# A written order of tasks for a sparse attention and expert kernel, with transposes of probabilities moved to SP from pair 23 on

## The chip, the cores and the metric

The kernel runs on one core of a Trainium2 chip. A core has TensorE (PE, matmuls, with weight loads shown as PEld), VectorE (DVE), ScalarE (ACT), GpSimd (POOL), and SyncE (SP), which here only issues DMAs. The engines run side by side, each in the order of its own program, and wait for each other through semaphores. Matmul results go to PSUM, which has eight banks of 128 x 512 fp32; everything else lies in SBUF or DRAM. The metric is the device time in microseconds, the median of several executions. Where one execution was profiled, its span runs from the first to the last instruction.

## The reference

Four batches of block-sparse attention with 8 heads, 768 positions in 24 blocks of 32, and head size 64, followed by one expert (an MLP) over all 3072 positions:

```python
mask = np.abs(blk_i - blk_j) <= 1
mask = mask | (blk_i == 0) | (blk_j == 0) | (blk_i == 23) | (blk_j == 23)
for qb in range(24):
    for kb in sampled_blocks[qb]:                 # three blocks per row of blocks
        mask[qb*32:(qb+1)*32, kb*32:(kb+1)*32] = True
attn = softmax(where(mask, q @ k.T / 8, -1e9));  x = attn @ v
h = x @ w_in                                      # 512 -> 2048
out = (h * sigmoid(beta * h)) @ w_out             # 2048 -> 512
```

So each of the 22 inner rows of blocks looks at 8 blocks: three sampled, its three neighbours, the first and the last. The first and the last row look at all 24.

## The kernel before

**Attention.** The inner rows are taken in pairs, 11 per batch, 44 in all. For pair n the kernel copies the sampled K blocks (task `kg`, six POOL copies with block numbers held in registers) and the neighbours (`kn`, on POOL or DVE) beside each other, multiplies with Q (`sc`, in 64x32 pieces of the array, the mask added first), takes maxima on DVE (`mx`, two tasks), exponentials with sums on ACT (`ex`, two tasks), normalises (`nrm`, four scalings, on POOL or DVE; for the first eleven pairs, `hl`, the scale is instead multiplied on later), transposes the probabilities (`tp` on PE and `ptv`, the copy out of PSUM) or, from pair 31 on, has SP do it by a transposing DMA (`tpd`), and multiplies with V (`av`, in halves of the array up to pair 15, on the whole array after that). `xv` brings the result into the expert's input xT. V's blocks come to SBUF by DMAs that SP issues (`vg`, with `vv` loading block numbers); for pairs 0 to 3 the sampled blocks are picked by matmul instead (`pick`, `pickv`). The first and last block rows of V are copied inside SBUF where possible (`vres`). The rows that look at everything are the tasks `gs`, `gm`, `ge`, `gr`, `gn`, `gt`, `gptv`, `gav`, `gx`.

**Preparing a batch.** q, k and v are loaded (`ld`), cast to fp16 for batch 0 (`castK`, `castQ`), transposed by PE (`trK`, `trQ`: six position groups times two heads, each a 128x64 piece) and copied out (`evK`, `evQ`). V is rearranged (`vperm`, `permV`) and written to a table in DRAM (`vtab`), from which `vg` gathers. The weights come by POOL's DMAs (`win`, `wout`).

**The expert** runs over eight groups G of 256 or 512 positions: `h` (16 tasks of four matmuls), `tanh` on ACT, `stt` on DVE into the buffer g, then `y` (four parts per 128 positions) and `oe`, `od`, which scale and store. The sigmoid is formed from tanh.

**What sets the order.** Each piece above is a Task (line 24) with engines it may run on, estimated durations, what it depends on, and the PSUM banks that it opens and closes. `Plan.run` (line 65) goes through time as a list scheduler: when an engine is free it takes the ready task of the lowest due time, plus a table of offsets by name, and for tasks with several engines the one that would end first, with two biases against DVE. It also hands out the banks and models two DMA queues. What it returns is one order, and the tasks are emitted in it (line 1226); each engine then executes its own in that order.

Lines that matter: `TD = (31, 1, 1)` at 266 (from which pair SP transposes), 528 to 540 (loads and casts of batch 0), 627 to 637 (transposes of K and Q), 704 (block numbers to POOL's registers, within `kg`), 841 (`vres`), 915 (`nrm`), 929 to 942 (`tp`, `ptv`, `tpd`), 1146 (which g buffer a group uses), 1198 to 1207 (the last output, scaled in halves by ACT and DVE).

Of the kernel before, what the change touches and what calls it, by code (L numbers as in the profile page):

```python
# [20 lines left out]
BIAS = {("nrm", "DVE"): 2.0, ("gn", "DVE"): 1.5}  # L21


class Task:
    def __init__(self, name, eng, dur, emit, deps=(), prio=0.0, lat=0.0,
                 opens=(), closes=(), moe=False, dma=0.0, slack=0.0, hw=0, bulk=None):
        self.on = {eng: dur} if isinstance(eng, str) else dict(eng)
        self.name, self.eng, self.dur, self.emit = name, None, None, emit
        self.deps = [d for d in deps if d is not None]
        self.prio, self.lat = prio, lat  # L30
        self.opens, self.closes, self.moe, self.dma = opens, closes, moe, dma
        self.slack, self.hw, self.bulk = slack, hw, bulk
        self.kind = name.rstrip("0123456789.")
        self.tiling = Plan.TILING.get(self.kind, 0)
        self.end = None


class Plan:


    HOP = 0.18
# [3 lines left out]
    MARGIN, DMARGIN = 1.0, 1.0  # L45


    TILING = {"sc": 1, "gs": 1, "av": 2, "gav": 2, "trK": 2, "trQ": 2}
    CHANGE, KEEP = 0.1, 0.0
    YOUNG = {"PE": 0, "DVE": 0, "ACT": 0.0, "POOL": 0.5, "SP": 0.0}  # L50
    YIELD = 20

    OFFSET = {'gt': 5, 'gav': 10, 'trK': 7.6, 'oe': 2.2, 'vg': -0.6, 'vv': -14.0, 'pick': -1.2, 'av0': 0.8, 'ptv0': -3.8, 'xv0': 3.7, 'vg0': 0.9, 'sc1': -2.5, 'kg1': 12.5, 'kn1': -11.1, 'mx1': -15, 'vg1': -5, 'av2': -5, 'kg2': 2.8, 'kn2': 4.2, 'hl2': 5.2, 'rs2': -5, 'kg3': -11.2, 'ex3': 0.3, 'rs3': -0.6, 'kg4': -15, 'rs4': 7.8, 'kn5': 18.1, 'ptv5': 6.3, 'rs5': 39.6, 'av6': -0.3, 'kg6': 2.5, 'kn6': -60, 'ptv6': -2.4, 'mx6': 4.5, 'sc7': 15.7, 'tp7': 21.7, 'av7': 1.3, 'rs7': 1.6, 'sc8': 0.4, 'hl8': -3.7, 'xv8': -17.7, 'av9': -14.9, 'kg9': -6.0, 'kn9': 15, 'mx9': -15, 'ex9': -0.6, 'hl9': 19.8, 'rs9': 15, 'sc10': 21.3, 'tp10': 0.8, 'av10': 15, 'kg10': 2.9, 'kn10': -15, 'mx10': 30, 'vg10': 30, 'sc11': -60, 'av11': 15, 'ex11': 5, 'xv11': -1.7, 'av12': 0.5, 'kn12': -2.5, 'ptv12': 1.2, 'rs12': -0.3, 'xv12': 26.5, 'tp13': -0.2, 'kn13': 4.0, 'rs13': -3.7, 'xv13': -41.1, 'av14': 15, 'kg14': -15, 'kn14': -30, 'rs14': 24.8, 'xv14': 6.6, 'ptv15': 30, 'xv15': -24.7, 'mx0.0': 0.7, 'mx0.1': -9.9, 'mx1.1': -3.1, 'ex1.1': 5.7, 'ex2.0': -2.1, 'ex4.1': -15, 'mx7.1': 56.3, 'gn1': -22.5, 'vperm0.0': -0.6, 'trQ1': 11.7, 'trQ2': 11.1, 'trK3': 2.2, 'trQ3': -0.4, 'castQ': 2.6, 'tabK2': -34.6, 'tabK3': 8.6, 'ttQ2': 19.9, 'ldV3': 0.9, 'pick1': 9.2, 'pickv': 30, 'ldV0.1': 0.1, 'evK0': -6.3, 'evQ0': -1.2, 'tanh0': 5.1, 'stt1': -14.2, 'h3': 0.5, 'y3': -1.4, 'oe3': -8.0, 'y4': 1.4, 'tanh4': 9.0, 'oe4': 1.7, 'h5': 15.9, 'y5': -1.2, 'stt5': 3.2, 'h6': -60, 'y6': 11.9, 'tanh7': 60, 'stt7': -19.4}

    def __init__(self, n_banks, moe_banks):
        self.tasks = []
        self.n_banks, self.moe_banks = n_banks, moe_banks
        self.bank = {}
# [6 lines left out]
    def run(self):  # L65
        tasks = self.tasks
        attention_left = sum(1 for t in tasks if t.opens and not t.moe)
        succ = {}
        need = {}
        for t in tasks:  # L70
            need[t] = len(t.deps)
            for d in t.deps:
                succ.setdefault(d, []).append(t)
        readers = {}
        for t in tasks:
            for b in t.closes:
                readers[b] = readers.get(b, 0) + 1
        ready_at = {t: 0.0 for t in tasks}
        engines = sorted({e for t in tasks for e in t.on})
        free = {e: 0.0 for e in engines}  # L80
        waiting = {e: [] for e in engines}
        ring_at = hw_at = 1.0
        lanes = [0.0] * 8
        issued = 0

        tiling = 0
        off = {t: t.prio + self.OFFSET.get(t.name, self.OFFSET.get(t.name.split(".")[0], self.OFFSET.get(t.kind, 0.0)))
               for t in tasks}

        def rank(t, e):  # L90

            young = now - ready_at[t] < self.YOUNG[e] - 1e-9
            return off[t] + (self.KEEP if e == "PE" and t.tiling != tiling else 0.0) + (self.YIELD if young else 0.0)

        bank_free = [(0.0, i) for i in range(self.n_banks)]
        held_moe = 0
        moe_owner = set()
        events = []
        seq = 0

        def release(t):
            for e in t.on:
                waiting[e].append(t)

        for t in tasks:
            if need[t] == 0:
                release(t)
        now = 0.0
        order = []
        done = 0  # L110
        while done < len(tasks):
            progress = False
            for e in engines:
                if free[e] > now + 1e-9:
                    continue
                best = None
                for t in waiting[e]:
                    if ready_at[t] > now + 1e-9:
                        continue
                    if len(t.on) > 1:  # L120
                        cost = {o: max(free[o], now) + d + BIAS.get((t.kind, o), 0.0)
                                for o, d in t.on.items()}
                        if cost[e] > min(cost.values()) + 1e-9:
                            continue
                    if t.bulk is not None and ring_at > now + t.bulk + 1e-9:
                        continue
                    if t.opens:
                        n_ok = sum(1 for f, _ in bank_free if f <= now + 1e-9)
                        if n_ok < len(t.opens):
                            continue  # L130
                        if t.moe and attention_left and held_moe + len(t.opens) > self.moe_banks:
                            continue
                    if best is None or rank(t, e) < rank(best, e):
                        best = t
                if best is None:
                    continue
                t = best
                for other in t.on:
                    waiting[other].remove(t)
                t.eng, t.dur = e, t.on[e] * (1.0 if e == "PE" else self.MARGIN)  # L140
                if e == "PE" and t.tiling != tiling:
                    t.dur += self.CHANGE
                    tiling = t.tiling
                if t.opens:
                    bank_free.sort()
                    for name in t.opens:
                        _, i = bank_free.pop(0)
                        self.bank[name] = i
# [1109 lines left out]
```

## Time and profile before

| | |
|---|---|
| runs | 304.17, 1516.72 and 300.63 us; median 304.17 |
| profiled execution | span 302.9 us; its own time is not recorded beside it |
| TensorE busy | 279.5 us (92%), 4109 matmuls |
| VectorE busy | 237.5 us (78%) |
| ScalarE busy | 218.6 us (72%) |
| GpSimd busy | 170.0 us (56%) |
| first score task, first h task, last matmul | at 23.4, 45.0 and 298.3 us |
| mean granted TensorE clock | 0.981 |
| DMA | 47.55 MB in 57170 packets, mean 157 GB/s |

Busy shares are averages over stages of different kinds; the prediction takes them apart by time. A group of instructions is shown with its line, its engine, what it writes and reads, the count, busy time and mean duration in ns, and then how long the engine had idled before it and for whom. In a timeline row the first number is the start, the second the length. Matmuls overlap, so the distance between starts tells more than the length. A line such as 330 is that of a copying helper, so the tiles' names tell the task.

### The profile page before, as it was taken

Reading aid. Unit: us, or ns where it says so; the run is one execution under the profiler, and the core shown is the slowest. Engines: PE = TensorE matmul, PEld = TensorE weight load, DVE = VectorE, ACT = ScalarE, POOL = GpSimd, SP = SyncE. Lnnn points to the kernel's source line nnn. Section 1 sums busy time; section 2 is a strip of 40 time slices with the busy share of each in tenths; the row PEclk is TensorE's granted clock in tenths of the full one; section 3 lists DMA queues with packets and bytes.
Section 4 is the critical chain, followed back from the end, with each engine's and each line's share of the span. In section 5 each row is a group of like instructions: output and inputs, shape, how many; then the busy total and the mean of one; then the engine's idle time right before and its main releaser. Section 6 shows DMA issues by size and latency. Waiting matters only on the chain.

```text
span 302.9 us, 11451 instructions
## 1 busy us (share of the span) xinstructions
PE 279.5 (92%) x4109; PEld 173.8 (57%) x4109; DVE 237.5 (78%) x556; ACT 218.6 (72%) x641; POOL 170.0 (56%) x513
## 2 busy tenths in 40 slices
PE   2599879999998799999999999999999999999993
PEld 1465668758846576665556555545554544555671
DVE  5848987999899998999999739999888834762150
ACT  3357657888789598799889749896787768763360
POOL 5057995034579957899777538677976654000000
PEclk9999957999999999999999999999999999999999
DMA  7999999979978852299933643248465446541102
GB/s 248 365 294 171 205 232 231 228 142 265 213 126 167 181 192 72 84 173 162 237 99 106 202 154 106 67 110 167 120 158 119 126 106 181 137 121 53 53 36 69
DMA packets 57170, 47.55 MB, mean 157 GB/s; under 512 B 19733, under 2 KB 53142, under 8 KB 57114
## 3 DMA queue, kind: packets, MB, share of 16 engines
q1 hardware_dynamic: 44736, 35.48, 41.3%
q0 software_dynamic: 12320, 11.27, 24.7%
q8 instruction: 32, 0.52, 0.7%
q14 instruction: 24, 0.20, 0.2%
q10 hardware_dynamic: 58, 0.07, 0.1%
HBM read 45.23 MB, written 9.44 MB: 180 GB/s over the span
## 4 chain that ended last, share of the span: by engine, by line
PE 49%; DVE 23%; issue 7%; ACT 6%; POOL 6%; DMA 5%; POOLq 2%; SPq 0%; DVEq 0%; ACTq 0%
PE bank L1155 17%; PE bank L1182 14%; DVE ST L884 5%; PE bank L825 4%; DVE g L1166 4%; PE bank L929 3%; POOL KG L710 3%; DMA g<-in_k_dram 3%; DVE SG L1040 3%; POOL PP L915 2%; PE bank L963 2%; PE bank L971 2%; ACT PP L892 2%; PE bank L632 2%; ACT t L1161 2%
## 5 line engine op out<-in xcount | busy, mean ns | idle before, releaser
L1155 PE MATMUL bank<-xT,w_in_sb 128*128 128x256 f16 (+1 forms) x512 | 93.8, 330 | 1.5 <-DVE g L1166 1.5
L892 ACT ACTIVATE PP<-bank,ST 128x256 f16<-128x256 f32 x176 | 81.9, 482 | 15.1 <-DVE ST L884 10.1
L1182 PE MATMUL bank<-w_out_sb,g 128*128 128x512 f16 x384 | 92.0, 379 | 0.0
L1161 ACT ACTIVATE t<-bank,beta_sb 128x512 f16<-128x512 f32 (+1 forms) x128 | 71.0, 595 | 15.7 <-PE bank L1155 10.4
L915 POOL TENSOR_SCALAR PP<-PP,ST 128x256 f16<-128x256 f16 x132 | 63.4, 499 | 30.8 <-DVE ST L909 29.2
L1166 DVE SCALAR_TENSOR_TENSOR g<-t,bank 128x512 f16<-128x512 f16 (+1 forms) x128 | 67.0, 547 | 16.3 <-ACT t L1161 15.8
L1155 PEld LDWEIGHTS <-w_in_sb 128*128 128x128 f16 x512 | 54.4, 115 | 28.1 <-issue 4.1
L710 POOL COPY KG<-KT 128x64 f32 x264 | 52.4, 249 | 25.6 <-PE bank L862 10.5
L884 DVE TENSOR_REDUCE ST<-bank 128x2 f32<-128x512 f32 x88 | 57.6, 680 | 4.2 <-PE bank L862 3.8
L1182 PEld LDWEIGHTS <-g 128*128 128x128 f16 x384 | 35.0, 98 | 37.4 <-issue 3.5
L892 ACT ACTIVATION_READ_ACCUMULATOR PP<-bank,ST 128x1 f32 x176 | 37.4, 212 | 0.0
L1061 POOL TENSOR_SCALAR PG<-PG,SG 128x768 f16<-128x768 f16 x13 | 13.1, 1010 | 24.4 <-ACT PG L1049 15.2
L334 ACT ACTIVATE osb<-bank 128x512 f32<-128x512 f32 (+1 forms) x24 | 14.2, 590 | 16.1 <-PE bank L1182 16.0
L330 DVE COPY PT<-bank 128x1024 f16<-128x1024 f16 x30 | 20.4, 683 | 3.8 <-PE bank L929 3.6
L330 DVE CAST xT<-bank 64x256 f16<-64x256 f32 (+1 forms) x35 | 14.6, 418 | 9.9 <-PE bank L963 6.8
L929 PE MATMUL bank<-identity,PP 128*128 128x128 f16 x248 | 20.4, 225 | 1.2 <-ACT KT L328 0.6
L963 PEld LDWEIGHTS <-VG 128*128 128x128 f16 x448 | 16.1, 98 | 9.2 <-issue 4.3
L1049 ACT ACTIVATE PG<-bank,SG 128x384 f16<-128x384 f32 x32 | 18.3, 589 | 4.2 <-DVE SG L1042 3.6
L929 PEld LDWEIGHTS <-PP 128*128 128x128 f16 x248 | 16.2, 101 | 6.0 <-issue 1.1
L963 PE MATMUL bank<-PT,VG 128*128 128x64 f16 x448 | 17.5, 193 | 2.2 <-DMA PT<-PP 1.5
L330 POOL COPY KG<-KT 128x384 f32<-128x384 f32 (+3 forms) x43 | 16.6, 411 | 1.3 <-PE bank L862 1.3
L328 ACT CAST xT<-bank 64x256 f16<-64x256 f32 (+1 forms) x30 | 11.3, 375 | 8.2 <-PE bank L1089 3.9
(119 smaller groups left out, 317.9 us busy)
## 6 DMA issues: line engine op xcount, KB each, us to landing
VG<-VT SPq DMA_DIRECT2D x220, 32.0 KB, 2.6
VG<-VT SPq DMA_DIRECT2D x32, 192.0 KB, 2.7
out_dram<-osb SPq DMA_DIRECT2D x20, 256.0 KB, 2.1
RV<-in_v_dram POOLq DMA_DIRECT2D x6, 384.0 KB, 6.6
RK<-in_k_dram POOLq DMA_DIRECT2D x6, 384.0 KB, 6.2
VT<-Vn SPq DMA_DIRECT2D x3, 768.0 KB, 3.4
RQ<-in_q_dram POOLq DMA_DIRECT2D x6, 384.0 KB, 6.3
w_in_sb<-in_moe_w_in_dram POOLq DMA_DIRECT2D x8, 256.0 KB, 8.8
```

Of the source, the lines that this page charges most:

```text
L330: (nc.vector if eng == "DVE" else nc.gpsimd).tensor_copy(out=out, in_=in_)
L710: nc.gpsimd.tensor_copy(out=kg32[:, g, :, (SR + r) * W:(SR + r + 1) * W], in_=kt32[:, :, bass.ds(vals[3 * g + r], W)])
L884: mx[n, u] = add(f"mx{n}.{u}", "DVE", 0.6, lambda n=n, u=u, sb_=sb_: nc.vector.tensor_reduce(out=sb_[:, 0, 2 * u:2 * u + 2], in_=bank(("S" ...
L892: nc.scalar.activation(out=pb[:, u, g, :], in_=bank(("S", n, u))[:, g * 256:(g + 1) * 256], func=AF.Exp, bias=sb_[:, 0, 2 * u + g:2 * u + ...
L915: (nc.vector if eng == "DVE" else nc.gpsimd).tensor_scalar(out=pb[:, u, g, :], in0=pb[:, u, g, :], scalar1=sb_[:, 2, 2 * u + g:2 * u + g + ...
L929: nc.tensor.transpose(out=o[:, s * P:(s + 1) * P], in_=pb[:, u, g, c * P:(c + 1) * P], identity=identity)
L963: nc.tensor.matmul(o[:, (g * NHP + hp) * 2 * BLK:(g * NHP + hp + 1) * 2 * BLK], lhsT=vgb[:, g, c, hp * P:(hp + 1) * P], rhs=pt[:, g, c, :, ...
L1049: nc.scalar.activation(out=pg[:, :].rearrange("x (j p) -> x j p", j=J)[:, :, hf * hw_:(hf + 1) * hw_], in_=bank(("GS", m, hf))[:, 0:S // 2 ...
L1155: nc.tensor.matmul(o[:, 0:TW], lhsT=w_in_v[:, c, f // 4, f % 4, :], rhs=xT[:, c, c0:c0 + TW], start=(c == 0), stop=(c == NHP - 1))
L1161: lambda G=G, f=f, TW=TW, tt=tt: nc.scalar.activation(out=tt[:, 0:TW], in_=bank(("H", G, f))[:, 0:TW], func=AF.Tanh, bias=0.0, scale=beta_ ...
L1166: lambda G=G, f=f, TW=TW, tt=tt, gg=gg: nc.vector.scalar_tensor_tensor(out=gg[:, f, 0:TW], in0=tt[:, 0:TW], scalar=1.0, in1=bank(("H", G, ...
L1182: nc.tensor.matmul(o[:, :], lhsT=gg[:, f, s * P:(s + 1) * P], rhs=w_out_sb[:, f, :], start=(f == 0), stop=(f == N_FFC - 1))
```

## The change

The list scheduler goes. `ORDER` is a text of 1726 task names; for tasks that may run on several engines a letter names it (A for ACT, D for DVE, G for POOL). `run` reads the tasks in this order and replays them against estimated durations, only to choose PSUM banks; the estimates are changed throughout (for instance 0.14 instead of 0.18 us for a hop between engines, 1.65 instead of 1.15 for `kg`). The planner's offsets, biases and limits on the expert's banks are gone. Besides:

- `TD = (23,1,1)`: SP transposes from pair 23 on, so `tp` and `ptv` of pairs 23 to 30 become `tpd`.
- The casts of batch 0 may run on ACT and put the heads of a pair side by side, so `trK` and `trQ` of batch 0 are six whole 128x128 transposes each. SP loads V, K, V, K, Q, Q by halves.
- The register loads for the sampled K blocks of pairs 0 to 3 become tasks of their own (`kl`), placed ahead of the copies.
- V's gather buffers are laid out with the two halves of a pair's keys outermost; w_in is loaded in eight pieces of one row group by half the columns, instead of two row groups by a quarter.
- G0 and G1 share one g buffer (columns 0 to 255 and 256 to 511); G2 takes the other.
- The last output is scaled by ACT alone.
- By engine: 11 `nrm` are on DVE (none before), `vres` 7 on POOL and 2 on DVE (all nine on DVE before), `kn` 36 on POOL and 8 on DVE (27 and 17), `ptv` 7 on ACT and 16 on DVE (1 and 30), `xv` 28 on ACT and 44 on DVE (26 and 46), `rs` 6 on ACT and 5 on DVE (9 and 2), batch 0's `castK` 3 on ACT, and two more evictions of Q on ACT.

```diff
+ORDER = """
+ident id32 selc sbl idx srow selb0 iota mask.0 ldV0.0 beta selb1 selw0 selw1 sel16.0 sel16.3 sel16.5 sel16.2 sel16.4
+vperm0.0 sel16.1 betaT ldK0.1 castK0.3:A trK0.3 castK0.2:A trK0.2 evK0.2:A ldV0.1 vperm0.1 pick0.1 pick1.1 ldK0.0
+castK0.0:A trK0.0 evK0.3:A castK0.1:D trK0.1 mask.1 mask.2 ldQ0.0 castQ0.1:D warm maskb maskc pick1.0 evK0.1:A
...
+od7.0 y7.1.1 y7.1.2 y7.1.3 oe7.1 od7.1ACT od7.1SP
+"""
...
+        by = {t.name: t for t in self.tasks}
+        full = dict(A="ACT", D="DVE", P="PE", G="POOL", S="SP")
+        order = []
+        for word in ORDER.split():
+            name, _, eng = word.partition(":")
+            t = by[name]
+            t.eng = full[eng] if eng else next(iter(t.on))
+            order.append(t)
...
-    TD = (31, 1, 1)
+    TD = (23,1,1)
...
-    VGs = sb("VG", [P, NVG, 2, 2, D_MODEL])
+    VGs = sb("VG", [P, 2, NVG, 2, D_MODEL])[:, :, :, :, :].rearrange("x c n g m -> x n g c m")
...
+    mixed = lambda t: t[:, :, :].rearrange("p h x -> p (h x)").rearrange("p (j m) -> p j m", j=J)
...
-                    f"cast{nm}0.{hp}", "DVE", 0.5,
-                    lambda i=i, dst=dst, hp=hp: nc.vector.tensor_copy(
-                        out=dst[:, 2 * hp:2 * hp + 2, :], in_=stage32(i, hp)),
+                    f"cast{nm}0.{hp}", {"DVE": 0.48, "ACT": 0.74}, None,
+                    lambda eng, i=i, dst=dst, hp=hp: copy_on(
+                        eng, mixed(dst)[:, :, hp * P:(hp + 1) * P].rearrange("p j (u d) -> p u j d", u=2),
+                        stage32(i, hp).rearrange("p u (j d) -> p u j d", j=J)),
...
+                    if b == 0:
+                        for j in range(J):
+                            nc.tensor.transpose(out=o[:, j * P:(j + 1) * P],
+                                                in_=mixed(s16)[:, j, hp * P:(hp + 1) * P], identity=identity)
+                        return
...
-        def emit_kg(n=n, b=b, p=p, kt32=kt32, kg32=kg32):
-            _, vals = nc.values_load_multi_w_load_instructions(
+        def emit_kl(n=n, p=p):
+            held_k[n] = nc.values_load_multi_w_load_instructions(
                 offP[0:1, p, 0:6], engines=(ET.Pool,), min_val=0, max_val=(NB - 1) * W,
+                skip_runtime_bounds_check_because="block numbers lie below the number of blocks")[1]
+        kl = add(f"kl{n}", "POOL", 0.45, emit_kl, deps=[t_idx, t_rc], prio=-1) if n < NKL else None
...
-        gi = (G + (sizes[0] < 8)) % NG if G or sizes[0] >= 8 else 0
-        gc = TW if G == 1 and sizes[0] < 8 else 0
+        gi, gc = ((0, 0), (0, 256), (1, 0), (0, 0), (1, 0), (0, 0), (1, 0), (0, 0))[G]
...
-                te.emit, te.on = lambda ob=ob, G=G, s=s: scale_on(
-                    "ACT", ob[:, 0:256], bank(("Y", G, s))[:, 0:256], 0.5), {"ACT": 0.35}
-                tf = add(f"of{G}.{s}", "DVE", 0.35, lambda ob=ob, G=G, s=s: scale_on(
-                    "DVE", ob[:, 256:512], bank(("Y", G, s))[:, 256:512], 0.5), deps=list(te.deps), prio=te.prio,
-                    closes=(("Y", G, s),))
```

452 lines of the change are left out of this document (245 added, 207 removed).

## The prediction

> **What bounds the kernel now.** I read the page's head and chain first, then the engines' busy time by stage.
>
> ```profile
> span 302.9 us, 11451 instructions
> PE 279.5 (92%) x4109; PEld 173.8 (57%) x4109; DVE 237.5 (78%) x556; ACT 218.6 (72%) x641; POOL 170.0 (56%) x513
> ...
> PE 49%; DVE 23%; issue 7%; ACT 6%; POOL 6%; DMA 5%; POOLq 2%; SPq 0%; DVEq 0%; ACTq 0%
> ```
>
> TensorE (PE) is busy 92% and is half of the chain; VectorE (DVE) is a quarter. An average hides the stages, so the next view cuts the span (columns: length, then busy time and count of each engine, granted clock, DMA).
>
> ```profile
> 0.00:10.00 10.00, 1.94 (x9) 1.06 (x9) 5.43 (x22) 2.44 (x4) 3.85 (x24) 1.00 0.80 279
> 24.00:45.00 21.00, 18.04 (x441) 12.97 (x420) 19.39 (x48) 14.91 (x57) 19.65 (x69) 0.85 1.11 201
> 45.00:94.00 49.00, 48.99 (x847) 34.86 (x846) 44.97 (x121) 40.40 (x125) 23.23 (x56) 0.96 1.01 201
> 94.00:107.00 13.00, 9.95 (x201) 7.71 (x199) 12.66 (x28) 9.14 (x29) 12.91 (x36) 1.00 0.82 168
> 107.00:298.30 191.30, 187.69 (x2476) 108.63 (x2470) 145.81 (x315) 144.36 (x418) 106.00 (x311) 1.00 0.50 125
> ```
>
> Four regimes: loads until about 10 us; a softmax stage (24 to 45) where DVE works 19.39 of 21 us; then PE nearly full to 298.3, with 0.01 + 3.05 + 3.61 = 6.7 us idle, half of it at 94 to 107, where DVE and POOL are full; and 302.9 - 298.3 = 4.6 us of last output. So after 45 us time is saved mainly by taking work off PE. Before it, DVE and the loads set the pace.
>
> **The change part by part.** *Shape switches on PE.* Score matmuls use 64x32 tiles, some transposes and value matmuls 128x64, the rest the whole array.
>
> ```profile
> 167.72 1.03 PE L1182 MATMUL bank<-w_out_sb,g 128*128 128x512 f16 x4
> 168.68 0.28 PE L849 MATMUL bank<-maskr,ones 64*32 64x192 f16 x8
> 168.77 0.40 PE L862 MATMUL bank<-KG,QT 64*32 64x256 f16 x16
> 169.10 1.04 PE L1182 MATMUL bank<-w_out_sb,g 128*128 128x512 f16 x4
> ...
> 170.31 1.03 PE L1182 MATMUL bank<-w_out_sb,g 128*128 128x512 f16 x4
> 171.18 0.63 PE L963 MATMUL bank<-PT,VG 128*128 128x64 f16 x16
> ```
>
> Four output matmuls before a full-array task take 171.18 - 170.31 = 0.87 us, before a score task 168.68 - 167.72 = 0.96: a switch costs about 0.1 us. Counting neighbours of different shape, PE's order before has 120 switches from the first expert matmul (h) on, the written list 76, since it puts score tasks beside each other, wide tasks too, and so on. 44 x 0.1 = 4.4 us off PE. Bounds: 0, where PE would wait anyway, and 4.4.
>
> *Pairs 23 to 30 transposed by SP.* Each drops eight PE transposes and one copy out of PSUM.
>
> ```profile
> 184.40 0.61 PE L929 MATMUL bank<-identity,PP 128*128 128x128 f16 x8
> 184.85 1.03 PE L1155 MATMUL bank<-xT,w_in_sb 128*128 128x512 f16 x4
> L330 DVE COPY PT<-bank 128x1024 f16<-128x1024 f16 x30 | 20.4, 683 | 3.8 <-PE bank L929 3.6
> PE bank L963 <- DMA PT<-PP: 1.5, 3, 0.7
> L933 SPq DMA_TRANSPOSE PT<-PP x13: 1232/1261/2792, 201.5 to 269.8; - x13
> DMA to landing us min/median/max: 2.7/2.8/4.2
> ```
>
> From start to start 0.45 us each: 8 x 0.45 = 3.6 us off PE, and 8 x 0.68 = 5.5 off DVE. Instead SP spends 1.26 us issuing and the data lands after 2.8, about 1.5 later than 0.61 + 0.68. What covers that is the PE work that the list puts between a pair's normalisation and its value matmul: from 3.0 us (pair 24: a score task and three output parts) to over 10. With a normalisation of 1.9 us the need is 4.7, so only pair 24 may be exposed, by up to 1.7 us; I take nothing. Behind a waiting transpose on SP stand gathers of V for the same and later pairs, and outputs; SP is in order. Without cover each pair loses the whole (the slow rival).
>
> *Work moved between DVE, ACT and POOL.* To DVE: 11 normalisations. From DVE: 14 copies of transposed probabilities (8 vanish, 6 go to ACT), 7 of 9 V edge copies and 9 of 17 K copies (to POOL), three opening casts and two Q evictions (to ACT).
>
> ```profile
> L915 POOL TENSOR_SCALAR PP<-PP,ST 128x256 f16<-128x256 f16 x132 | 63.4, 499 | 30.8 <-DVE ST L909 29.2 <-DVE SG L1057 1.3
> L1061 DVE TENSOR_SCALAR PG<-PG,SG 128x768 f16<-128x768 f16 x3 | 1.9, 640 | 0.0
> L330 DVE COPY KG<-KT 128x768 f16<-128x768 f16 x17 | 7.4, 434 | 0.0
> L330 DVE COPY VG<-VG 32x2048 f16<-32x2048 f16 x9 | 6.9, 770 | 0.2
> L328 ACT COPY PT<-bank 128x1024 f16<-128x1024 f16 x1 | 1.0, 1020 | 0.0
> L336 DVE TENSOR_SCALAR QT<-bank 128x768 f16<-128x768 f16 x5 | 4.8, 955 | 3.4 <-PE bank L632 3.4
> ```
>
> No row shows the probabilities' normalisation on DVE, or a V edge copy on POOL. The first: below, a third of 640 per piece (0.85 for four); above, four times 434 (1.7); I take 0.9, nearest to the same operation. The second: below, 0.77 as on DVE; above, eight pieces of 499 ns (4.0) for its 2048 elements; I take 2.0, in between, for want of a nearer row. DVE then: +11 x 0.9 - 14 x 0.68 - 7 x 0.77 - 9 x 0.43 - two evictions of 0.95 and three casts of some 0.55 (-3.6; a pair of casts takes 1.07 in the opening's rows below) = -12 (bounds -13 to -4); POOL: -11 x 1.9 + 7 x 2.0 + 9 x 0.5 = -2 (bounds -11 to +12); ACT: +6 x 1.02 and as much again in small pieces, up to +10, on an engine that idles 47 us of the last long stretch. On PE this can show only where PE waits: of the 3.05 us idle at 94 to 107 I take half back, 1.5 (bounds: all 6.7 of idle gained, or 6 lost in new waits, as much as is there now).
>
> *The opening.* SP's order becomes V, K, V, K, Q, Q; casts go to ACT, heads side by side make six full transposes instead of twelve halves; two picks (gathers of V by matmul) go ahead of two of the four K transposes.
>
> ```profile
> 9.20 2.73 SPq L528 DMA_DIRECT2D g<-in_q_dram  x1
> 18.37 1.07 DVE L538 CAST RQ<-g 128x768 f16<-128x768 f32 x2 [0.21 <-DMA g<-in_q_dram]
> 23.43 0.33 PE L849 MATMUL bank<-maskr,ones 64*32 64x320 f16 x8
> 44.98 1.90 PE L1155 MATMUL bank<-xT,w_in_sb 128*128 128x256 f16 x8
> L884 DVE TENSOR_REDUCE ST<-bank 128x2 f32<-128x512 f32 x14 | 9.1, 681 | 1.1 <-PE bank L862 1.1
> L334 ACT ACTIVATE QT<-bank 128x768 f16<-128x768 f16 x11 | 8.8, 832 | 1.6 <-PE bank L632 1.6
> ```
>
> The loads move the same bytes, so the last Q half still lands at about 18.4. From there to the first score task the kernel takes 5.0 us: casts, then PE still on picks, then evictions, the last on DVE. The list lets the transposes follow the casts at once and gives two late evictions to ACT: cast 1.1, transpose 0.4, evictions 0.8 each, about 21.5 rather than 23.4. Registers for pairs 0 to 3 are loaded while POOL waits for K, so they cost nothing, and the copies of K start without them. The picks wait for the second half of V, and behind them on PE stand the other two K transposes; their K half lands later than that V half, so nothing is late for it. From the first score task on DVE binds: up to the value outputs of pair 3, on which the first h task waits, the list gives DVE 16 maxima of 0.65 (9.1 / 14) and about 10 us of other work (copies of probabilities and picks, reciprocals, evictions, two K copies, a global maximum), 20.5 in all. Back to back that is 42.0; with the 1.6 us that DVE idles in 24 to 45 now, 43.5. So h starts 1.5 us earlier (bounds: 3 earlier, 1 later if POOL's K copies or the weights are late). Less attention work is done by then (pair 4's transposes and value task and a score task open, another score and a global one done): +0.8 on PE afterwards.
>
> *The clock.* The granted clock falls in this stage:
>
> ```profile
> 37.00:38.00 1.00, 0.36 (x3) 0.09 (x2) 0.93 (x4) 1.00 (x5) 1.00 (x5) 1.00 1.16 294
> 38.00:39.00 1.00, 0.00 (x0) 0.00 (x0) 1.00 (x3) 0.83 (x4) 1.00 (x3) 0.84 1.19 240
> 48.00:49.00 1.00, 1.00 (x17) 0.76 (x12) 0.64 (x3) 0.69 (x3) 1.00 (x2) 0.54 1.13 238
> ```
>
> Half speed from 38.7 to 48.9, of which 3.9 us lie in the h stage: about 2 us lost. The list leaves three picks instead of four to fill PE in this wait, so PE idles as much there; I change nothing (bounds: 2 gained, 3 lost).
> [...]
>
> *Small things.*
>
> ```profile
> L334 ACT ACTIVATE osb<-bank x24: 384/597/629, 62.8 to 298.3; 128x512 f32<-128x512 f32 x23, 128x256 f32<-128x256 f32 x1
> ```
>
> The last output is scaled whole by ACT, 0.6 us, instead of half each by ACT and DVE, 0.4: +0.2. Storing G0 and G1 side by side in one g buffer frees G1 from waiting for V of pairs 4 to 7; PE was full there, so nothing. Banks are given out by the list's own replay; a bad one makes PE wait for an eviction, which is part of the 6 us bound above. The new V layout, weight pieces of other shape and touches cost what they did, beside full engines.
>
> **The sum**: 302.9 - 1.5 (opening) - 4.4 (switches) - 3.6 (transposes) + 0.8 - 1.5 (waits) + 0.2 = 292.9 us of span. The median of the runs shown, 304.17, is 1.3 above the profiled span, and the lowest of them, 300.63, lies 1.2% below it: so 294.2, and 2% is about what a measurement of this kernel can tell from no change.
>
> **Rivals.** *More comes off* (0.22): the clock stays full and all waits go. -2 and another -3.5 of idle: 288.7. For it: DVE is relieved. Against: the softmax stage stays bound by DVE.
>
> *The relief turns into locking* (0.18): DVE and POOL slow each other.
>
> ```profile
> 90.42 2.83 POOL L915 TENSOR_SCALAR PP<-PP,ST 128x256 f16<-128x256 f16 x4
> 94.03 1.84 POOL L915 TENSOR_SCALAR PP<-PP,ST 128x256 f16<-128x256 f16 x4
> ```
>
> Four pieces took 2.83 us while DVE ran two V edge copies (the group of 770 ns above), else 1.84. With 11 normalisations on DVE, each of four pieces that may stand behind POOL's long copies, the pairs' chains lengthen by 1 to 2 us and the 8 us off PE return as waits: 302.9 - 1.5 + 1.3 = about 302.5. It decides where a chain has less than that to spare.
> [...]
>
> *Transposes by SP exposed* (0.10, slower): if SP reaches them late, because gathers ahead wait for buffers, each of the eight pairs loses its 2.8 and one issue of 1.26 ahead of it, less the 1.3 that PE and DVE took: 2.8 us, 22 in all on 294.2; with a fifth of it beside other waits, about 312. Against: for the thirteen transposes of before PE waited 1.5 us in all, 0.7 at most. It decides where SP is more than 3 us late at most of the eight. That the list is not followed as written is no rival of its own: engines run it in order.
>
> **Chances.** The forecast, 0.5, own range 291 to 298; the rivals as given. Below 298.1 lie nine tenths of the forecast's case and the first rival: faster 0.67. Within 2%: the lock and the rest: 0.23. Slower 0.10. The range, 287 to 304, takes in both outer rivals but the slow one.
>
> **What would show it.** First score task near 21.5, first h near 43.5; PE's count down by 64 transposes and 48 half-transposes and its busy time by 9 us or more; waits after h not above 6; SP's 21 transposes landing in 2.8 with little PE wait. Wrong if PE idles more than 12 us after h, if DVE's scaling pieces take over 0.5, or if h starts after 46.

## The result, and the profile after

The changed kernel takes 314.46 us (median; 311.8 to 316.76) against 302.4 us, a ratio of 1.037 with a 95% interval of 1.025 to 1.049. The prediction was 294.2, with 287 to 304 as its range. Medians here are over all executions, ratios and their intervals leave out those that a slower state of the chip lengthened, so the two need not agree to the last per cent. The changed kernel's profiled execution took 315.78 us, with a span of 314.0.

The head of the page after, span and TensorE's line:

```profile
span 314.0 us, 11136 instructions
...
PE 274.4 (87%) x3997; PEld 171.3 (55%) x3997; DVE 223.8 (71%) x556; ACT 225.1 (72%) x651; POOL 164.6 (52%) x494
```

PE's work did fall, by 5.1 us (279.5 to 274.4), and the span grew by 11.1: so PE idles 16.2 us more. The view by stages tells where (columns as in the prediction: length, busy time and count of PE, PEld, DVE, ACT and POOL, granted clock, DMA share, GB/s). First two stretches of before that the prediction ran together with others:

```profile
150.00:200.00 50.00, 49.32 (x748) 28.30 (x746) 42.18 (x92) 40.88 (x120) 31.46 (x94) 1.00 0.44 126
200.00:260.00 60.00, 57.75 (x719) 30.44 (x720) 45.83 (x101) 46.27 (x145) 39.62 (x112) 1.00 0.56 138
```

and the stretches of after:

```profile
24.00:45.00 21.00, 16.18 (x376) 10.45 (x374) 16.34 (x44) 16.52 (x63) 15.63 (x58) 0.84 0.98 186
45.00:94.00 49.00, 45.73 (x883) 34.92 (x878) 42.76 (x119) 41.78 (x129) 31.36 (x88) 0.97 0.99 193
94.00:107.00 13.00, 10.08 (x248) 7.67 (x243) 7.67 (x17) 8.72 (x33) 8.46 (x15) 0.87 0.92 174
...
107.00:150.00 43.00, 38.64 (x668) 25.60 (x667) 37.40 (x95) 37.08 (x111) 33.08 (x101) 1.00 0.57 136
150.00:200.00 50.00, 43.24 (x635) 24.86 (x634) 36.48 (x86) 39.69 (x117) 33.24 (x94) 1.00 0.85 161
200.00:260.00 60.00, 56.29 (x700) 29.45 (x699) 46.00 (x102) 43.48 (x134) 27.82 (x88) 1.00 0.61 138
```

PE stands still 6.76 us at 150 to 200 (before 0.68), 4.36 at 107 to 150, 3.71 at 200 to 260, 3.27 at 45 to 94. No other engine is full in those stretches: DVE, which the change relieved, works 36.48 of 50 us. The DMA engines' share at 150 to 200 doubled, from 0.44 to 0.85.

PE's waits in the trace after (line waited at, engine and tile waited for: total us, times, longest):

```profile
PE bank L1018 <- DMA VG<-VT: 9.2, 8, 2.9
...
PE bank L916 <- issue: 2.9, 1, 2.9
...
PE bank L916 <- POOL KG L370: 1.8, 1, 1.8
PE bank L1018 <- issue: 1.7, 1, 1.7
```

Line 1018 is the value task `av` on the whole array. By these rows it waits for gathered V, which no row of before has among its waits. So something that SP issues is late. Two of the stalls on PE's timeline, and what SP did before the first (start, length, what, how many; idle before and for whom):

```profile
128.64 1.09 PE L1018 MATMUL bank<-PT,VG 128*128 128x64 f16 x32 [1.84 <-DMA VG<-VT]
169.72 0.63 PE L1018 MATMUL bank<-PT,VG 128*128 128x64 f16 x16 [2.90 <-DMA VG<-VT]
```

```profile
116.01 12.46 SPq L864 DMA_DIRECT2D VG<-VT  x19
```

The profile puts a wait for several DMAs down to the one that it takes for the last, and at the second stall that is the wrong one. By the semaphore updates in the trace, pair 24's last gather had landed at 167.24 and its transposed probabilities landed at 169.58, just before the value task started. In the same way the stall at 157.60 (pair 23, 1.87 us) ended 0.13 us after the landing of SP's transpose, and the one that the row above calls issue (193.46, pair 28, 1.70 us) 0.09 us after it. So some 6.5 us at line 1018 waited for transposes by SP (pairs 23, 24 and 28), and 3.3 us for gathers alone (1.84 at pair 18, 1.44 at pair 21).

Laying the list beside SP's instructions in order names the gathers. Pair 18's last gather was issued at 124.44, for the value tasks at 128.64, and 17 of the 19 gathers above were for pairs 18, 19 and 20 in mixed order. In before a pair's gathers stand together, pair after pair. How long before its `av` a pair's last gather had been issued shows the change best: 13.2, 12.8, 10.2 and 8.9 us for pairs 31 to 34 before, and 1.5, 1.5, 1.2 and 1.8 after. SP's lead is gone.

The same comparison for the eight pairs that the change gave to SP: from the end of the normalisation to the start of the transpose's issue 5.1, 5.2, 5.4, 4.0, 3.4, 6.2, 5.4 and 3.0 us pass. That is the point that the prediction set for its slow rival ("more than 3 us late at most of the eight").

### The profile page after: what moved, and what is told of

Its sections match the earlier page's. It is cut to its first block, busy times and chain, and to the rows that moved or that the text cites. A ratio compares the mean times of both kernels' runs of the same rounds, so it can differ in the third digit from the quotient of the medians.

```text
span 314.0 us, 11136 instructions
## 1 busy us (share of the span) xinstructions
PE 274.4 (87%) x3997; PEld 171.3 (55%) x3997; DVE 223.8 (71%) x556; ACT 225.1 (72%) x651; POOL 164.6 (52%) x494
## 2 busy tenths in 40 slices
DMA packets 64593, 49.63 MB, mean 158 GB/s; under 512 B 28181, under 2 KB 59542, under 8 KB 64538
## 5 line engine op out<-in xcount | busy, mean ns | idle before, releaser
L1210 PE MATMUL bank<-xT,w_in_sb 128*128 128x256 f16 (+1 forms) x512 | 95.6, 333 | 2.3 <-ACT PP L947 1.5
L1210 PEld LDWEIGHTS <-w_in_sb 128*128 128x128 f16 x512 | 55.4, 116 | 29.5 <-issue 3.3
L970 POOL TENSOR_SCALAR PP<-PP,ST 128x256 f16<-128x256 f16 x88 | 41.2, 484 | 44.2 <-DVE ST L964 43.9
L939 DVE TENSOR_REDUCE ST<-bank 128x2 f32<-128x512 f32 x88 | 56.9, 682 | 10.2 <-PE bank L916 10.0
L370 POOL COPY KG<-KT 128x384 f32<-128x384 f32 (+3 forms) x62 | 22.9, 404 | 14.7 <-ACT KT L368 10.5
L1018 PE MATMUL bank<-PT,VG 128*128 128x64 f16 x448 | 18.4, 193 | 13.2 <-DMA VG<-VT 9.2
L1018 PEld LDWEIGHTS <-VG 128*128 128x128 f16 x448 | 16.2, 98 | 20.5 <-issue 12.9
L374 ACT ACTIVATE osb<-bank 128x512 f32<-128x512 f32 x24 | 14.4, 599 | 14.4 <-PE bank L1237 12.2
L370 DVE CAST xT<-bank 64x256 f16<-64x256 f32 (+1 forms) x33 | 13.6, 418 | 10.9 <-ACT xT L368 6.2
L916 PE MATMUL bank<-KG,QT 64*32 64x256 f16 x704 | 16.9, 275 | 4.7 <-issue 2.9
L1096 DVE TENSOR_REDUCE SG<-bank 128x1 f32<-128x384 f32 x32 | 16.2, 547 | 1.7 <-PE bank L1082 1.7
L984 PE MATMUL bank<-identity,PP 128*128 128x128 f16 x184 | 14.9, 227 | 1.6 <-ACT PP L947 1.0
L984 PEld LDWEIGHTS <-PP 128*128 128x128 f16 x184 | 12.1, 101 | 5.7 <-issue 3.4
```

What stands on the lines that cost most here:

```text
L370: (nc.vector if eng == "DVE" else nc.gpsimd).tensor_copy(out=out, in_=in_)
L939: mx[n, u] = add(f"mx{n}.{u}", "DVE", 0.6, lambda n=n, u=u, sb_=sb_: nc.vector.tensor_reduce(out=sb_[:, 0, 2 * u:2 * u + 2], in_=bank(("S" ...
L970: (nc.vector if eng == "DVE" else nc.gpsimd).tensor_scalar(out=pb[:, u, g, :], in0=pb[:, u, g, :], scalar1=sb_[:, 2, 2 * u + g:2 * u + g + ...
L984: nc.tensor.transpose(out=o[:, s * P:(s + 1) * P], in_=pb[:, u, g, c * P:(c + 1) * P], identity=identity)
L1018: nc.tensor.matmul(o[:, (g * NHP + hp) * 2 * BLK:(g * NHP + hp + 1) * 2 * BLK], lhsT=vgb[:, g, c, hp * P:(hp + 1) * P], rhs=pt[:, g, c, :, ...
L1210: nc.tensor.matmul(o[:, 0:TW], lhsT=w_in_v[:, c, f // 4, f % 4, :], rhs=xT[:, c, c0:c0 + TW], start=(c == 0), stop=(c == NHP - 1))
```

## The experiments

Four theories. **A**: the list scatters the gathers, and SP, in order, is stopped by a later pair's gather in front of an earlier pair's. **B**: the eight transposes on SP cost the time. **C**: DVE and POOL are in each other's way after the moves. **D**: opening stage and clock.

### Order and transposes, one by one and together

Sorted gathers (within `ORDER`; 228 words move), e1:

```diff
-... vg15.5 vg15.4 vg15.2 vg17.4 vg17.0 vg17.3 ...
+... the same places, filled pair by pair as far as dependencies allow
```

> The changed kernel, and only the gathers of V from pair 12 on dealt out anew: the same places in the written list, filled in the order of the pairs (228 of them move). Theory A (the list scatters a pair's gathers, so SP, in order, waits with a later pair's gather in front of an earlier pair's last one, and the value tasks wait for V): the 9.2 us that PE waits for VG go, about 306 us. Theory B (the eight more transposes by SP hold the probabilities' buffers and take SP's time): less than 2 us of change, 312 to 315. Theory C (DVE and POOL in each other's way after the moves) and theory D (opening stage and clock): no change, 314.

PE's transposes again, e2, and both, e3:

```diff
-    TD = (23,1,1)
+    TD = (31,1,1)
-... tpd23 ... tpd30 ...
+... tp23 ptv23:D ... tp30 ptv30:D ...
```

> The changed kernel with pairs 23 to 30 transposed by PE and copied by DVE again, the copies of the list otherwise as written. A: PE gets 8 x 0.45 = 3.6 us more, SP loses 8 x 1.26 us of issuing, the scattered gathers stay: 311 to 316. B: the 9.8 us that ACT waits for the transposing DMA go, and with them most of the loss against before: 304 to 308. C and D: 3.6 more work on PE, 316 to 318.

> Both edits at once: gathers in the order of pairs, and pairs 23 to 30 transposed by PE. A: as with sorted gathers alone, plus up to 3.6 of PE, 306 to 309. B: as with PE's transposes alone. If both count, about 302; if neither (C, D), 314 to 318.

And the transposes alone, in the kernel before, whose planner is left as it was, e4:

```diff
-    TD = (31, 1, 1)
+    TD = (23, 1, 1)
```

> The kernel before, its planner unchanged, and only the first pair that SP transposes put from 31 to 23. A: the eight transposes are harmless where each pair's gathers stand together: 299 to 303 (3.6 us off PE, some of it back in waits). B: they cost by themselves: 306 to 310.

| kernel | median us | ratio to before (95%) |
|---|---|---|
| e1, gathers sorted | 311.77 | 1.031 (1.024 to 1.039) |
| e2, PE's transposes | 310.1 | no interval |
| e3, both | 304.39 | 1.007 (1.004 to 1.011) |
| e4, before with SP's transposes | 316.19 | 1.047 (1.040 to 1.054) |

e2's four times lie between 307.1 and 312.6 us, too far apart for an interval.

e4 is the surprise: the eight transposes without the rest of the change cost the old kernel 13.7 us, as much as the whole change. (The planner plans anew with them, so the order of later tasks differs from before's too.) A alone missed (2.7 us of the 8 expected), B alone missed (4.4 of 8), but together they give back 10.1 of 12.1 us. They are two loads on one resource. In e1 the waits for V vanish, and at its pair 23 PE instead waits 3.6 us at the value task, 4.6 us after SP had finished issuing that pair's transpose. C and D, which expected no change, can hold only the 2.0 us that are left of the loss; of the gain that was forecast they can hold more.

Where e4 loses it: PE's wait at the value tasks, and SP's timeline.

```profile
PE bank L963 <- DMA PT<-PP: 14.3, 7, 5.3
```

```profile
201.58 1.28 SPq L933 DMA_TRANSPOSE PT<-PP  x1
204.01 4.39 SPq L810 DMA_DIRECT2D VG<-VT  x9
208.51 1.26 SPq L933 DMA_TRANSPOSE PT<-PP  x1
209.86 0.53 SPq L1214 DMA_DIRECT2D out_dram<-osb  x1
210.49 1.31 SPq L1216 DMA_DIRECT2D out_dram<-osb  x1
211.85 0.42 SPq L1217 DMA_DIRECT2D out_dram<-osb  x1
212.37 4.14 SPq L810 DMA_DIRECT2D VG<-VT  x9
216.62 1.97 SPq L933 DMA_TRANSPOSE PT<-PP  x1
```

SP issues without a pause but for the gap at 202.9, in which it loads registers for 1.05 us. Nine gathers take 4.4 us, a transpose 1.3 or more, outputs 0.4 to 2.3, and these transposes start 6.9 and 8.1 us apart; the kernel before needs a pair every 5.8 us (value tasks of pairs 23 to 43 from 157.8 to 273.4). Further on, with seven gathers a pair, the transposes of pairs 36 to 40 of e4 start 5.7 us apart (236.2 to 258.8), just the pace that is needed, so a delay of SP is never made good.

### Is it SP's time, or the transposes' delay?

Theory **F**: SP's time. Theory **G**: a transpose's own delay (1.26 of issue, some 3 to land). The first try was to take the outputs of groups 1 to 5 off SP:

```diff
-    NBP, ODP, RP = 99, (), 0
+    NBP, ODP, RP = 99, (1, 2, 3, 4, 5), 0
```

in the changed kernel (e5), in e4 (e6, where the planner plans anew), in e1 (e7) and in e3 (e8).

> The changed kernel with the outputs of groups 1 to 5 issued by POOL instead of SP (16 tasks, some of two DMAs, about 9 us of SP's issuing and its waits for the scaled output); the list as written. Theory F (SP's issuing time is what has run out: nine gathers a pair at 0.45, one transpose at 1.26 and an output leave it no lead, so each us put on SP is a us later for every pair behind): 306 to 310. Theory G (a transpose costs by its own delay, issue 1.26 and landing 3, wherever SP is not late): 312 to 316.

> The kernel before with SP transposing from pair 23 on, and the outputs of groups 1 to 5 issued by POOL. F: most of the 13.7 us that the eight transposes cost there come back, 303 to 309. G: 314 to 318.

> The changed kernel with the gathers of V in the order of pairs and the outputs of groups 1 to 5 issued by POOL; the eight transposes stay with SP. F: 302 to 307, as good as with PE's transposes. G: 309 to 313.

> Gathers in the order of pairs, pairs 23 to 30 transposed by PE, outputs of groups 1 to 5 issued by POOL. F: SP has some lead already with the first two edits, so little more, 301 to 304.5. G: no change against the first two edits, 304 to 305.

Measured 316.49, 315.46, 317.47 and 312.86 us: none gained beyond a microsecond, and e7 and e8 lost 5.7 and 8.5. These runs don't decide between F and G, because the outputs now leave late: POOL, in order too, waits for them, and the output buffers come free later, so that ACT and behind it PE wait (POOL's waits in e8, then PE's, which account for 3.8 of the 8.5 us):

```profile
POOL out_dram L1264 <- ACT osb L374: 12.1, 1, 12.1
```

```profile
PE bank L1125 <- ACT osb L374: 3.8, 1, 3.8
```

A cleaner pair of tests puts load on SP, or takes it off, and touches no other engine. e9 adds load to the kernel before, same order, behind a pair's last gather:

```diff
+                if 23 <= n < 31 and k_ == last_:
+                    for x_ in range(3):
+                        c_ = (3 * (n - 23) + x_) * 4
+                        nc.sync.dma_start(out=dum[:, c_:c_ + 4], in_=vt[0:BLK, 0:4])
```

> The kernel before, same order, no transpose moved; at the end of the gathers of each of pairs 23 to 30 SP issues three more tiny DMAs (32 rows of 8 bytes into a tile that nobody reads), 24 in all, some 0.45 us of SP's time each, so about 1.35 a pair, as much as one transpose's issue. Theory F (SP's issuing time is what has run out): slower by 6 us or more, up to 11. Theory G (the transposes' own delay): no change, within 2 us.

It took 311.71 us, 1.028 (1.021 to 1.035): 9.0 us for 24 DMAs of 0.41 us (256 bytes each) that nobody waits for. The row of the added DMAs, SP's timeline, and PE's in e9:

```profile
L815 SPq DMA_DIRECT2D dum<-VT x24: 311/414/1298, 150.3 to 194.0; - x24
```

```profile
193.03 1.40 SPq L815 DMA_DIRECT2D dum<-VT  x3
195.31 12.86 SPq L811 DMA_DIRECT2D VG<-VT  x23
208.28 1.36 SPq L938 DMA_TRANSPOSE PT<-PP  x1
```

```profile
211.60 1.01 PE L968 MATMUL bank<-PT,VG 128*128 128x64 f16 x16 [8.96 <-DMA PT<-PP]
```

and SP's timeline at that place in before:

```profile
179.50 20.48 SPq L810 DMA_DIRECT2D VG<-VT  x33
...
200.07 1.31 SPq L810 DMA_DIRECT2D VG<-VT  x3
201.48 1.37 SPq L933 DMA_TRANSPOSE PT<-PP  x1
```

The load was put at 150 to 194, where PE didn't notice it. It was paid in one piece, 8.96 us, when pair 31's transpose, the first of before, came to its turn behind the gathers: 208.28 instead of 201.48. SP had issued back to back from 179.5 on already in before. So a debt of SP's time alone, with no transpose moved, costs what F says.

The opposite, from pair 23 on: one gather of fixed blocks for six of sampled ones, the same bytes (five issues and their register loads off SP), in the kernel before (e10), in e4 (e11), in the changed kernel (e12) and in e1 (e13); and in e3 (e17). These five leave out the sampled choice of V, so their output is another one; they serve only to tell the causes apart.

```diff
+            if n >= 23 and k_ >= len(ms_) - 6:
+                f = None if k_ > len(ms_) - 6 else lambda v, vgb=vgb, vt=vt: (
+                    vgb[0:3 * BLK, :, 0, :],
+                    bass.AP(tensor=vt.tensor, offset=vt.offset + BLK * D_MODEL,
+                            ap=[[D_MODEL, 3 * BLK], [BLK * D_MODEL, 2], [1, D_MODEL]]))
```

> The kernel before, same order; for pairs from 23 on the six gathers of sampled V blocks are one DMA of the same bytes from fixed blocks (so the sampled choice of V is left out there), which takes five issues, 2.2 us a pair, off SP. F and G both: 0 to 3 us faster, as PE waits little there; it is the control for the next two.

> The kernel before with SP transposing from pair 23 on, and from pair 23 on one gather of fixed blocks of V in place of six of sampled ones. F: the 13.7 us are gone, 297 to 303, no slower than the control. G: 310 to 316.

> The changed kernel, list as written, and from pair 23 on one gather of fixed blocks of V in place of six of sampled ones; a pair's one gather stands where the first sampled one stood. F: the loss after 150 us goes, what is left is the opening, the stall at 96 to 99 and the waits for V up to pair 22: 302 to 307. G: 311 to 315.

> The changed kernel with the gathers of V from pair 12 on in the order of pairs, and from pair 23 on one gather of fixed blocks in place of six: SP has room everywhere. If SP's time and order are the whole loss, what is left is the change's gain on PE against the control of before with one gather (299.8): 293 to 297. If the opening and the stall at 96 to 99 give the gain back: 297 to 301.

> Gathers in the order of pairs, one gather of fixed blocks from pair 23 on, and pairs 23 to 30 transposed by PE; to be set beside the same with SP's transposes (298.5). If the eight transposes by SP do take 3.6 us off PE once SP has room: 301 to 303. If their delay of some 4.5 us costs as much as they save: 297.5 to 300.

| kernel, SP relieved | median us | without the relief | ratio to before (95%) |
|---|---|---|---|
| e10, before | 299.81 | 302.74 | 0.993 (0.987 to 0.998) |
| e11, before with SP's transposes | 306.19 | 316.19 | 1.011 (1.006 to 1.017) |
| e12, changed | 301.56 | 314.46 | 0.988 (0.982 to 0.995) |
| e13, changed, gathers sorted | 298.54 | 311.77 | 0.980 (0.973 to 0.987) |
| e17, changed, sorted, PE's transposes | 303.06 | 304.39 | 1.001 (0.996 to 1.005) |

The relief is worth 2.9 us to before, 10.0 to e4, 12.9 to the changed kernel and 13.2 to e1: F for the written list. For e11 F expected 297 to 303, and its 306.19 lies between the two theories. In e13 PE is full again where the changed kernel stood still, though the DMA engines' share is as high as there (0.86):

```profile
150.00:200.00 50.00, 49.05 (x755) 28.73 (x755) 42.06 (x96) 42.07 (x122) 35.50 (x110) 1.00 0.86 189
200.00:260.00 60.00, 59.96 (x651) 32.29 (x650) 48.64 (x115) 46.46 (x140) 29.11 (x80) 1.00 0.55 136
```

SP's lateness shows the cause directly. From the end of the normalisation to the start of the transpose's issue, pairs 23 to 30 take 0.6, 0.0, 0.0, 0.0, 1.2, 0.1, 0.0 and 0.0 us in e13, where the changed kernel took 3.0 to 6.2. From issue to landing they take 2.7 to 6.9 us in e13 and 2.8 to 7.7 in the changed kernel (2.7 to 4.2 for the thirteen of before). So the transfers were slow in both, and PE waited only where SP came late as well: neither the DMA engines' share nor the transposes' small packets (28181 packets under 512 bytes in the changed kernel, 19733 in before) held PE by themselves.

e13 and e17 differ in the eight transposes alone. With room on SP they are worth having in the written list: 4.5 us by the medians and 2.1% by the ratios, more than the 3.6 us predicted. PE's busy time in e13 and in e17:

```profile
PE 274.2 (92%) x3997; PEld 171.9 (58%) x3997; DVE 226.0 (76%) x556; ACT 224.1 (75%) x651; POOL 163.9 (55%) x494
```

```profile
PE 276.8 (92%) x4061; PEld 174.2 (58%) x4061; DVE 230.0 (76%) x564; ACT 224.6 (75%) x651; POOL 164.1 (55%) x494
```

Even so e13 is only 1.3 us below its control e10 by the medians, and 1.3% (some 4 us) by the ratios, whose intervals meet at 0.987. Its 298.54 lies where the opening and the stall at 96 to 99 were expected to give the gain back (297 to 301). In the planner's order the transposes don't pay: e11 stays 6.4 us above e10. The planner lays out all later pairs anew there, and which part of that costs the 6.4 stays open.

### The stall that no semaphore ends, and the opening

In the changed kernel and in e1 to e3 PE stands still for 2.5 to 3.1 us in the middle of a score task, near 96 us. e15 puts three parts of output matmuls between the short matmuls ahead of it (on e3):

```diff
-... av11 ... gav0 ... sc15 ... sc16 ... y1.0.3 oe1.0 ... y1.1.0 ... y1.1.1
+... av11 ... y1.0.3 oe1.0 gav0 ... y1.1.0 sc15 ... y1.1.1 sc16 ...
```

> Gathers sorted and pairs 23 to 30 transposed by PE (304.4), and three parts of output matmuls moved forward, between the short matmuls of 92 to 99 us (one before gav0, one before sc15, one before sc16). If the stall of 2.5 us in the middle of a score task, which no semaphore ends, is PE's instructions running out after some 300 short matmuls in 7 us: it falls below 0.5 and the clock's fall behind it too, 301 to 303. If it is a hidden wait for data: it moves or stays, 304 to 306.

PE's timeline in e3, and then in e15:

```profile
91.68 1.20 PE L1026 MATMUL bank<-PT,VG 128*64 128x32 f16 x64
92.70 0.95 PE L1145 MATMUL bank<-PTG,Vn 128*64 128x64 f16 x48
...
93.98 0.40 PE L916 MATMUL bank<-KG,QT 64*32 64x256 f16 x15
96.88 0.28 PE L916 MATMUL bank<-KG,QT 64*32 64x256 f16 x1 [2.50 <-issue]
```

```profile
96.49 1.04 PE L1237 MATMUL bank<-w_out_sb,g 128*128 128x512 f16 x4
97.46 0.28 PE L903 MATMUL bank<-maskr,ones 64*32 64x192 f16 x8
97.55 0.40 PE L916 MATMUL bank<-KG,QT 64*32 64x256 f16 x16
97.89 0.62 PE L984 MATMUL bank<-identity,PP 128*128 128x128 f16 x8
```

The stall is gone, and the granted clock at 94 to 107, 0.87 in e3, is 1.00 in e15. The time is 301.14 us, 0.995 (0.991 to 0.999), 3.3 us less than e3's. With e16 and e18 below (0.995 each) it is the best of the kernels that leave nothing out, ahead of before by little more than the measurement can tell.

That 211 matmuls in 4.3 us (from 90.13 on in e3; the expectation's 300 was a guess) empty PE's supply of instructions is the author's reading; no run shows that supply itself, but the DMA packets in the traces agree with it. One of the queues that the profile marks as instruction, in e3:

```profile
q8 instruction: 32, 0.52, 0.8%
```

Its 32 packets of 16 KB go with 8122 matmuls and weight loads of PE in e3, which would be some 250 to a packet if they all were PE's, an estimate. One of them starts at 94.33 us, as PE comes to stand (94.38), and ends at 95.64; PE goes on at 96.88, 1.24 us later. In the changed kernel the packet lasts from 96.53 to 97.49, and PE goes on at 98.79, 1.30 us later. Eleven of the kernels have this stall (2.3 to 3.1 us). In each of them such a packet is on its way during the stall, and PE goes on 1.2 to 1.4 us after its end. In e15 the packet comes at the same place (94.87 to 95.95), and there PE has output matmuls to work on (from 95.10 on). Why the packet doesn't come earlier no run shows.

For the opening, e14 moves the K copy of pair 3 from POOL to DVE on e3, e16 adds that to e15, and e18 adds the four pieces of w_in's first half ahead of other weights:

```diff
-... ptv0:D sc2 ... kn3:G sc3 ...
+... ptv0:D kn3:D sc2 ... sc3 ...
-... wout0.1 ... win1.1 ... wout1.1 win0.0 wout3.0 ... win0.3
+... win0.0 ... win0.3 ... wout0.1 win1.1 wout1.1 ... wout3.0
```

> Gathers sorted and pairs 23 to 30 transposed by PE (304.4), and the K copy of pair 3 on DVE, ahead of the maxima of pair 2, instead of on POOL behind weight transfers. If PE's wait of 1.5 to 1.8 us for that copy is what lets the clock fall at 28 us and holds up the opening: the clock stays up to 35 us, the first h comes 1.5 to 3 us earlier, 301.5 to 303. If not: 304 to 305.

> Both of the last two edits on the kernel with sorted gathers and PE's transposes. If both causes hold: 299 to 301.5, faster than before. If neither: 304 to 305.

> Sorted gathers, PE's transposes, the K copy of pair 3 on DVE, output parts between the short matmuls, and on POOL the four first-half pieces of w_in ahead of pieces that the first h tasks don't need. If the weights' landing is what took over at the first h (1.6 to 1.7 us of PE's wait there): first h near 44, 299 to 300.5, faster than before by 1%. If DVE's queue holds it anyway: 301 to 302.

They took 304.62 (0.999, 0.994 to 1.004), 301.62 (0.995, 0.991 to 0.999) and 301.33 us (0.995, 0.991 to 0.998), and by the medians that changes nothing beside e3 and e15. By the ratios e14 is 0.9% below e3, and their intervals just touch. The clock's fall at 28 us is gone in e14 (its first fall is at 43.8), but in e17, whose opening is e3's, too. The first h came at 44.4 in e14 and at 45.8 in e3, but at 44.6 in e17: it varies by over a microsecond from one execution to the next, and single profiles can't tell this edit from that. What holds the opening stays open.

## Why the prediction was wrong

**Transposes by SP, "I take nothing" for their cover, and the waits term of -1.5.** This step failed. The working counted the PE work between a pair's normalisation and its value task, and took SP to be there when the normalisation ends. It quoted SP's order ("SP is in order") but never added up SP's time: some 4.4 us of gathers, 1.3 for a transpose and an output, against 5.8 us a pair. In before, SP's issues and register loads already fill 39.8 us of 150 to 200 and 53.1 of 200 to 260. SP came 3.0 to 6.2 us late at all eight (at most 1.2 in e13, where it has room), and PE's idle time went up by 16.2 us where 1.5 was taken off: some 6.5 at the value tasks of pairs 23, 24 and 28, 3.3 at the gathers of pairs 18 and 21, and 2.9 in the stall near 96 us. The landing after 2.8 us was too short as well, 2.8 to 7.7 at the eight, but e13 bears such flights without a wait. The bound that was given for it, 6 us of new waits "as much as is there now", had no mechanism behind it. The slow rival had the right place, the right limit (3 us) and nearly the right time (312), but the wrong reason, gathers that wait for buffers, and a chance of 0.10. Its evidence against, that PE waited only 1.5 us for the thirteen transposes of before, came from a stretch that SP entered with 10 us of lead; e9 shows the lead being spent and then 8.96 us paid at the first of them. Of the signs that were to show a wrong prediction two came: PE idles 21.4 us from the first h to the last matmul (12 was the limit, before has 6.6), and h starts after 46. PE's busy time fell by 5.1 us, not by 9 or more.

**What was left of the gain.** The sum had 292.9 for the span. e13, with SP relieved and the gathers in order, has 297.3, still 4.4 above it, and it owes some of that to the relief, which alone is worth 2.9 us to before (e10): beside that control the change gained 1.3 us by the medians, of 10 forecast. Its first h comes at 46.98, 3.5 later than forecast, and its stall near 96 us takes 3.1; how much of the 4.4 is either's was not told apart.

**The scattered gathers** were seen ("gathers of V for the same and later pairs") and not priced. Sorting them gave back 2.7 us while SP had the eight transposes (e1), and 5.7 by the medians once PE had them again (e2 to e3; e2's times are far apart).

**Eight transposes off PE, -3.6.** The term holds where SP has room: 2.6 us less busy time and 4.5 us less time from e17 to e13.

**Shape switches, -4.4.** Right in sign; the size stays open. The traces have 120 switches from the first h on in before and 78 in after (76 counted). e3 has the regrouping and no transpose moved, and PE's busy time is 2.1 us below before's, 2.7 in e17. That time includes stretches at half clock, 9.4 us of it in before, 13.5 in e3 and 10.0 in e17; with these counted half, an estimate, the differences are 4.1 and 3.0. The merged transposes of batch 0 are in them too, so the switches' own share was not told apart.

**The opening, -1.5.** Failed: the first score task came at 22.50 rather than 21.5 and the first h at 46.87 rather than 43.5, later than the 46 that was to tell. The term ran DVE back to back from the first score task; it waited 4.0 us for score tasks instead (DVE's waits at 24 to 47, then PE's timeline):

```profile
DVE ST L939 <- PE bank L916: 4.0, 2, 2.5
```

```profile
28.78 0.63 PE L916 MATMUL bank<-KG,QT 64*32 64x256 f16 x16 [1.77 <-POOL KG L370]
...
30.73 1.94 PE L879 MATMUL bank<-Vn,xT 128*96 128x512 f16 x4
```

The K copy of pair 3, moved to POOL, stands behind weight transfers there (POOL issues one from 27.69 on, for 0.53 us, and copies from 28.21 on); then the clock has fallen (at 28.22, to 0.5), and four pick matmuls take 1.94 us where the four at 23.28 took 1.06. The prediction's bound of 1 us later, "if POOL's K copies or the weights are late", was too narrow.

**The clock, unchanged.** It fell three times, for 6.8, 3.4 and 3.4 us (from 28.2, 55.5 and 99.9), where before it fell once at work, for 10.2. The third fall follows the stall of 2.92 us and went with it in e15.
In the 3.4 us before the three falls (as long as the two shorter falls lasted) PE stood still for some 2.2, 1.6 and 2.3 us and worked the rest; in before it stood still for 2.0 of the 3.4 us before the fall at 38.7. By what rule the clock falls no run shows.

**Work moved between engines, and the locking rival.** The sizes came out: DVE 13.7 us less (12 predicted), POOL 5.4 less (2), ACT 6.5 more (up to 10). The rows of after:

```profile
L970 DVE TENSOR_SCALAR PP<-PP,ST 128x256 f16<-128x256 f16 x44 | 11.5, 329 | 0.2
...
L970 POOL TENSOR_SCALAR PP<-PP,ST 128x256 f16<-128x256 f16 x88 | 41.2, 484 | 44.2 <-DVE ST L964 43.9 <-DVE SG L1113 0.3
L370 POOL COPY VG<-VG 32x2048 f16<-32x2048 f16 x7 | 13.4, 1924 | 0.5 <-POOL KG L370 0.3
```

Four pieces on DVE take 0.87 to 1.72 us in its timeline, 0.93 as the middle of the eleven (0.9 taken; the mean of 329 ns counts overlaps twice). An edge copy on POOL takes 1.92 (2.0 taken). POOL's pieces didn't slow (499 to 484 ns). A slowing such as the locking rival had in mind shows clearly once, in the slowest four (POOL's row, then DVE's):

```profile
223.85 1.90 POOL L370 COPY VG<-VG 32x2048 f16<-32x2048 f16 x1
224.69 1.72 DVE L970 TENSOR_SCALAR PP<-PP,ST 128x256 f16<-128x256 f16 x4
```

The first of these pieces took 1.14 us, where the middle of all is 0.28, and ended 0.08 us after POOL's edge copy. That is some 0.9 us once, far from the loss; whether a lock is behind it no run shows. (The rival's own sum comes to 302.7, not 302.5.) Relief of DVE bought nothing, since PE didn't wait for DVE but for SP.

**The last output, +0.2.** From the last matmul to the end 4.5 us, against 4.6: nothing.

## What to carry to other kernels

Add up the issuing time of a queue like SP as one adds up an engine's busy time, per pair or per tile, before giving it more work: a queue that only issues shows as no engine in a busy table, and it can be nearly full all the same (53 of 60 us here, at 200 to 260 in before). The lead with which loads are issued ahead of their use is a stock; work added in one stage spends it without a trace, and the bill comes in a later stage, at the first thing on that queue that has no lead (in e9, 24 issues at 150 to 194 were paid with 8.96 us of PE's wait that ended at 211.6). Two loads on one such queue must be tested together, since undoing either alone gave back 2.7 and 4.4 us of 12.1, and both 10.1.

## What the runs showed of the hardware

- 24 DMAs of 256 bytes, each with a 0.41 us issue on SP, cost 9.0 us: issuing, not bytes, was the price.
- A transposing DMA of 128 x 1024 fp16 takes 1.26 us to issue (the median of thirteen in before). Eight of them raise the DMA engines' share at 150 to 200 from 0.48 (e17) to 0.86 (e13), with no loss on PE while SP has room (busy 49.05 of 50 us in e13, 48.51 in e17).
- PE stood still for 2.3 to 3.1 us after some two hundred short matmuls on end (211 in e3), with no wait that the profile shows, and went on 1.2 to 1.4 us after the end of a packet of instructions. It didn't stand still when long matmuls stood between the short ones (e15, from 93.25 on).
